# Reading wq in whole rows, a sigmoid on ScalarE and a bf16 residual in a decode kernel bound by its loads

## The chip, the cores and the metric

One core of one Trainium2 chip, the neighbouring cores idle. The metric is the device time of one execution in microseconds; lower is better. Executions of one kernel here spread by about 1%, so small differences are read from the traces (where the bytes were at what moment) and only totals from the timed runs.

## The reference, cut to what matters

Four tokens (batch 4, one position) pass twice through an attention layer and a gated layer, with residuals:

```python
def A(x, k_cache, v_cache, wq, wo):           # x after layer norm, [4, 512]
    q = x @ wq                                # wq: [512, 4096], bf16; 32 heads of 128
    k, v = last 2048 positions of the caches  # 8 kv heads, 4 query heads share one
    p = softmax(q @ k.T * 128**-0.5)
    return (p @ v) @ wo
def B(x, w_gate, w_up, w_down):               # 512 -> 1792 -> 512
    return (sigmoid(x @ w_gate) * (x @ w_up)) @ w_down
x = x + A(norm(x)); x = x + B(norm(x)); x = x + A(norm(x)); x = x + B(norm(x))
```

The same weights and caches serve both rounds. All of it, with what is read twice, comes to 72.36 MB of loads.

## The kernel before

All loads go through one queue (SyncE) into an arena of 50 slots of 512 KB (128 partitions x 4 KB). Each load takes a free slot; a slot comes free when the last instruction that reads it is done. The instructions of the five engines are planned by a list scheduler at build time; semaphores follow from that plan. K stays in the arena between the two attention layers, V and the weights are read again.

```python
wq_d = A_wq.rearrange("(kt p) n -> p kt n", p=128)      # block c: rows 128c .. 128c+127
...
# one load: half of each of 128 rows: 4 KB out of every 8 KB
chunk_load[("wq", c, i)] = lambda n, c=c, i=i: load_cols(
    n, wq_d[:, c, i * SLOT:(i + 1) * SLOT], SLOT, "bw_4k")
WQ_CH = [("wq", c, i) for i in range(2) for c in range(NC)]   # i outer: block 0,1,2,3 of half 0, then of half 1
...
def q_proj(k, b0, b1):
    for i in ((0, 1) if k == 0 else (1, 0)):                  # the query in two halves of 16 heads
        for c in range(NC):
            s = use_w("wq", k, ("wq", c, i))
            ...  # 4 matmuls of block c, half i; then done_w: the slot is free
        ...      # transpose, scale, replicate half i
...
# gated layer: sigmoid = 1 / (1 + exp(-g))
activation(egv, tv, ACTF.Exp, scale=-1.0)                     # ScalarE
tensor_scalar(eg, eg, 1.0, None, ALU.add)                     # VectorE
reciprocal(eg, eg)                                            # VectorE
tensor_tensor(hT, tv, egv, ALU.mult)                          # VectorE: times the up projection
...
# end: residual in f32, cast, transpose, copy, store
tensor_tensor(xT, ps, xT, ALU.add)
tensor_copy(xn, xT)                                           # the cast to bf16
```

## Time and profile before

| | before |
|---|---|
| timed, median (range, runs) | 192.74 us (192.09 to 193.40, 4) |
| profiled span | 190.2 us |
| loads | 72.36 MB; the load queue holds its 16 engines 97.9% of the span |
| busy share PE, DVE, ACT | 54%, 46%, 18% |

The span is the time on the core between first and last record; the timed figure is some 2 us longer. The profile's rows of slices cut the span into 40 parts; the row that matters here is the one of bytes per second. It stands under 400 where the packets are small (wo, in rows of 1 KB), it dips in the second slice and in the 27th, where the two passes over wq begin, and less in the 25th (371), where weights of the gated layer are read:

```profile
GB/s 133 344 416 410 408 410 389 409 394 404 407 390 411 391 405 412 388 409 394 400 393 389 407 405 371 397 337 409 409 409 408 402 410 406 408 408 405 403 365 16
```

Beside the profile's views I use one measure that comes from the packet records of the trace: the moment by which so many MB had arrived, counted from the first packet of the input x ("44 MB at 112.03 us").

### The profile page before, as it was taken

The numbers are of one execution on the slowest core, as the hardware profiler recorded it, in microseconds if no ns is written. First come the engines' busy times: TensorE is split into PE (matmuls) and PEld (weight loads), VectorE is DVE, ScalarE is ACT, GpSimd is POOL, SyncE is SP. The second block draws the span as 40 slices with busy tenths as digits, with TensorE's granted clock in tenths as the row PEclk, the third lists the DMA queues.
The fourth block names the chain that finished last, engine by engine and source line by source line (L and its number), as shares of the span: only waits on it lengthen the run. The fifth ranks groups of instructions, "written<-read, shape, count | busy, mean of one in ns | idle before, by whom it ended". The sixth has DMA issues, their size and how long they took to land.

```text
span 190.2 us, 4466 instructions
## 1 busy us (share of the span) xinstructions
PE 103.1 (54%) x1920; PEld 58.0 (30%) x1920; DVE 88.3 (46%) x220; ACT 33.3 (18%) x91; POOL 13.8 (7%) x73
## 2 busy tenths in 40 slices
PE   0443322655517264171654436445979999966543
PEld 0110000232404123041234331321355555655122
DVE  6136998486582854729410023122584443311421
ACT  2010011430303003030020000000373333310100
POOL 3000001110101001010010000000022111100000
PEclk9999999999999999999999999999995555555555
DMA  4999999999999999999999999999999999999990
GB/s 133 344 416 410 408 410 389 409 394 404 407 390 411 391 405 412 388 409 394 400 393 389 407 405 371 397 337 409 409 409 408 402 410 406 408 408 405 403 365 16
DMA packets 23412, 72.66 MB, mean 382 GB/s; under 512 B 2264, under 2 KB 6368, under 8 KB 23392
## 3 DMA queue, kind: packets, MB, share of 16 engines
q1 hardware_dynamic: 23392, 72.37, 97.9%
q8 instruction: 15, 0.25, 0.5%
q14 instruction: 5, 0.04, 0.1%
HBM read 72.36 MB, written 0.00 MB: 381 GB/s over the span
## 4 chain that ended last, share of the span: by engine, by line
SPq 52%; DMA 29%; PE 10%; issue 4%; DVE 3%; ACT 2%; ACTq 0%
SPq L369 51%; DMA arena<-in_A_v_cache_dram 13%; DMA arena<-in_B_w_down_dram 11%; DMA arena<-in_A_wq_dram 5%; PE ps L653 3%; PE ps L718 2%; ACT prow L670 1%; PE ps L808 1%; PE ps L679 1%; PE ps L840 1%; DVE nmax L661 1%; PE ps L580 1%; PE ps L748 1%; DVE ebuf L684 0%; DVE ebuf L588 0%
## 5 line engine op out<-in xcount | busy, mean ns | idle before, releaser
L653 PE MATMUL ps<-arena,qbd 128*16 128x512 bf16 x256 | 28.7, 594 | 30.3 <-DVE arena L633 26.5
L718 PE MATMUL ps<-ebuf,arena 128*128 128x4 bf16 x1024 | 34.3, 167 | 15.6 <-DMA arena<-in_A_v_cache_dram 10.9
L633 DVE STREAM_TRANSPOSE arena<-arena 128x1024 f32<-128x1024 f32 x32 | 38.6, 1226 | 0.6 <-DMA arena<-in_A_k_cache_dram 0.2
L718 PEld LDWEIGHTS ps<-ebuf,arena 128*128 128x128 bf16 x1024 | 31.4, 104 | 23.8 <-DMA arena<-in_A_v_cache_dram 21.8
L670 ACT ACTIVATE prow<-ps,nmax 128x512 bf16<-128x512 f32 x16 | 13.3, 829 | 42.7 <-DVE nmax L667 41.3
L653 PEld LDWEIGHTS ps<-arena,qbd 128*16 128x16 bf16 x256 | 6.4, 109 | 44.1 <-DVE arena L633 27.1
L730 DVE TENSOR_TENSOR onb<-ps,rinv 128x16 bf16<-128x16 f32 x16 | 3.1, 192 | 35.5 <-PE ps L718 35.4
L661 DVE TENSOR_REDUCE nmax<-ps 128x1 f32<-128x512 f32 x16 | 10.9, 683 | 15.3 <-PE ps L653 15.3
L621 ACT CAST qbd<-ps 32x64 bf16<-32x64 f32 x32 | 6.5, 203 | 48.7 <-DVE qbd L618 48.4
L580 PE MATMUL ps<-arena,xn 128*4 128x512 bf16 x64 | 9.3, 576 | 9.4 <-DMA arena<-in_A_wq_dram 6.5
L688 POOL CAST s<-psm 128x1 bf16<-128x1 f32 x16 | 3.0, 187 | 146.9 <-ACT prow L670 146.9
L679 PE MATMUL ps<-prow,perm 128*128 128x512 bf16 x16 | 9.0, 563 | 5.4 <-ACT prow L670 5.2
L681 ACT CAST prow<-ps 128x512 bf16<-128x512 f32 x16 | 9.4, 586 | 9.5 <-PE ps L679 9.5
L684 DVE STREAM_TRANSPOSE ebuf<-prow 128x256 f32<-128x256 f32 x16 | 7.1, 442 | 8.4 <-ACT prow L681 8.3
L748 PE MATMUL ps<-onb,arena 128*128 128x4 bf16 x256 | 9.3, 166 | 2.9 <-DVE onb L730 1.5
L808 PE MATMUL ps<-arena,xn 128*4 128x448 bf16 x64 | 7.3, 556 | 6.4 <-DMA arena<-in_B_w_up_dram 3.5
L618 DVE CAST qbd<-ps 32x64 bf16<-32x64 f32 x32 | 6.8, 212 | 5.1 <-ACT qbd L621 3.8
L748 PEld LDWEIGHTS ps<-onb,arena 128*128 128x128 bf16 x256 | 8.2, 104 | 3.2 <-issue 2.9
L547 ACT ACTIVATE lnv<-lnv 128x4 f32<-128x4 f32 x4 | 0.8, 206 | 39.3 <-DVE lnv L544 39.3
L588 DVE STREAM_TRANSPOSE ebuf<-ps 128x512 f32<-128x512 f32 x4 | 2.9, 714 | 9.8 <-PE ps L580 9.8
L840 PE MATMUL ps<-hT,arena 128*128 128x4 bf16 x112 | 4.2, 167 | 4.3 <-DVE hT L830 2.2
L815 DVE STREAM_TRANSPOSE ebuf<-ps 128x448 f32<-128x448 f32 x4 | 2.6, 650 | 7.9 <-PE ps L808 7.9
(55 smaller groups left out, 61.8 us busy)
## 6 DMA issues: line engine op xcount, KB each, us to landing
arena<-in_A_v_cache_dram SPq DMA_DIRECT2D x61, 512.0 KB, 12.6
arena<-in_A_k_cache_dram SPq DMA_DIRECT2D x32, 512.0 KB, 13.1
arena<-in_A_wq_dram SPq DMA_DIRECT2D x16, 512.0 KB, 8.6
arena<-in_A_wo_dram SPq DMA_DIRECT2D x8, 512.0 KB, 15.0
arena<-in_B_w_gate_dram SPq DMA_DIRECT2D x8, 448.0 KB, 13.9
arena<-in_B_w_up_dram SPq DMA_DIRECT2D x8, 448.0 KB, 13.7
arena<-in_B_w_down_dram SPq DMA_DIRECT2D x6, 512.0 KB, 10.2
arena<-in_B_w_down_dram SPq DMA_DIRECT2D x2, 256.0 KB, 10.3
```

What stands on the lines that cost most here:

```text
L369: o = P.op("sync", name, 0.0, lambda e, dst=dst, src=src: e.dma_start(dst, src), r=r, w=w, dma_bytes=nbytes, dma_rate=tm[rate])
L580: last = pe.matmul(ps[32 * hh:32 * hh + NB, qb, :], xn[:, c * NB:(c + 1) * NB], slot_ap(s)[:, hh * 512:(hh + 1) * 512], start=(c == 0), st ...
L633: P.op("vector", "T%d_%d" % (h, b), c_dve(1024), lambda v, v32=v32: v.transpose(v32, v32), r=[("slot", s)], w=[("slot", s)])
L653: last = pe.matmul(ps[32 * gi:32 * gi + NR, bank, :], qbd[:, q0:q0 + NR], kt[:, cp // 2, cp % 2, :, :], start=(cp == 0), stop=(cp == 3))
L661: lambda v: v.tensor_reduce(nmax[:, k2:k2 + 1], ps[:, bank, :], AXX, ALU.max),
L670: lambda a: a.activation(prow[:, :].rearrange("p (j k t) -> p j t k", k=32, t=2), ps[:, bank, :].rearrange("p (j t k) -> p j t k", k=32, t ...
L679: lambda pe: pe.matmul(ps[:, PB, :], perm[:, :], prow[:, :], start=True, stop=True),
L681: P.op("scalar", "pc" + tag, c_act(512), lambda a: a.copy(prow[:, :], ps[:, PB, :]), r=[("ppb",)], w=[("prow",)], banks=(PB,))
L684: lambda v: v.transpose(ebuf[:, k2 * 256:(k2 + 1) * 256], prow[:, :].bitcast(F32)),
L718: last = pe.matmul(ps[:, ob, gi * REP:(gi + 1) * REP], src[:, j * 128:(j + 1) * 128], ev[:, j % 2, j // 2, gi * REP:(gi + 1) * REP], start ...
L748: last = pe.matmul(ps[:, wb, c * nb:(c + 1) * nb], slot_ap(s)[:, r_ * D + c * 128:r_ * D + (c + 1) * 128], ov[:, o0:o0 + nb], start=(first ...
L808: last = pe.matmul(ps[32 * g:32 * g + NB, SB[n], 0:NF], xn[:, c * NB:(c + 1) * NB], slot_ap(s)[:, g * NF:(g + 1) * NF], start=(c == 0), st ...
```

## The change

The first pass over wq reads whole rows (8 KB) into two neighbouring slots, four loads of 1 MB in place of eight of 512 KB; the second pass stays as it was. The sigmoid becomes Exp, Ln(1 + .), Exp(-.), all on ScalarE. The last residual add writes bf16 directly, so the cast goes. The planner no longer counts a semaphore delay between two TensorE operations, which moves a few matmuls in the plan. (A field `lazy` is added to the planner and is zero everywhere.)

```diff
-                    td = d.finish + sem_lat
+                    td = d.finish + (0.0 if e == "tensor" and d.eng == e else sem_lat)
...
+        def load_wq_rows(c):
+            def emit(s):
+                assert pool.alloc() == s + 1
+                where[(("wq", c, 1), 0)] = s + 1
+                o = s * SLOT
+                dma("wqr%d" % c, arena[:, o:o + 2 * SLOT], wq_d[:, c, :], w=[("slot", s), ("slot", s + 1)],
+                    rate="bw_8k")
+            loads.append(((("wq", c, 0), 0), emit))
...
+            if kind == "wq" and k == 0:
+                for c in range(NC):
+                    load_wq_rows(c)
+                return
...
-            P.op("vector", "gp1%d" % k, c_dve(NH),
-                 lambda v: v.tensor_scalar(eg[:, 0:NH], eg[:, 0:NH], 1.0, None, ALU.add),
+            P.op("scalar", "gln%d" % k, c_act(NH),
+                 lambda a: a.activation(eg[:, 0:NH], eg[:, 0:NH], ACTF.Ln, bias=1.0),
...
-            P.op("vector", "grc%d" % k, c_dve(NH) + 250.0,
-                 lambda v: v.reciprocal(eg[:, 0:NH], eg[:, 0:NH]),
+            P.op("scalar", "grc%d" % k, c_act(NH),
+                 lambda a: a.activation(eg[:, 0:NH], eg[:, 0:NH], ACTF.Exp, scale=-1.0),
...
+            if last:
+                P.op("vector", "gres%d" % k, tm["dve_fix"] + 40.0,
+                     lambda v: v.tensor_tensor(xn[:, :], ps[:, CB, 128:128 + NX], xT[:, 0:NX], ALU.add),
+                     r=[("cb",)] + xts, w=[("xn",)], banks=(CB,))
+                return
...
-        P.op("vector", "out_cast", tm["dve_small"], lambda v: v.tensor_copy(xn[:, :], xT[:, 0:NX]),
-             r=[("xT", b) for b in range(NB)], w=[("xn",)])
```

More of the change, by code (lines that the diff above doesn't have):

```diff
@@ L17 @@
     __slots__ = ("idx", "eng", "name", "dur", "emit", "deps", "users", "start", "finish",
-                 "sem", "val", "inc", "dma_bytes", "dma_rate", "waits", "prio", "ndeps_left")
+                 "sem", "val", "inc", "dma_bytes", "dma_rate", "waits", "prio", "ndeps_left", "lazy")
     def __init__(self, idx, eng, name, dur, emit):
@@ L37, in __init__ @@
         self.ndeps_left = 0
+        self.lazy = 0.0
 class _Plan:
@@ L47, in __init__, with op @@
         self.bank_prev = {}
-    def op(self, eng, name, dur, emit, r=(), w=(), banks=(), dma_bytes=0, dma_rate=0.0, after=()):
+    def op(self, eng, name, dur, emit, r=(), w=(), banks=(), dma_bytes=0, dma_rate=0.0, after=(), lazy=0.0):
         o = _Op(len(self.ops), eng, name, dur, emit)
+        o.lazy = lazy
         o.dma_bytes = dma_bytes
@@ L125, in _schedule @@
                 ests.append((t, o))
-                if tmin is None or t < tmin:
-                    tmin = t
+                if tmin is None or t + o.lazy < tmin:
+                    tmin = t + o.lazy
             pick = None
             for x in ests:
-                if x[0] <= tmin + tol and (pick is None or x[1].prio < pick[1].prio):
+                if x[0] + x[1].lazy <= tmin + tol and (pick is None or x[1].prio < pick[1].prio):
                     pick = x
-            key = (pick[0], pick[1].prio)
+            key = (pick[0] + pick[1].lazy, pick[1].prio)
             if best is None or key < best_key:
@@ L263 @@
     dma_issue=60.0, dma_lat0=900.0, dma_lat1=1100.0, dma_max_out=16,
-    bw_4k=412.0, bw_3k=409.0, bw_1k=356.0,
+    bw_8k=430.0, bw_4k=412.0, bw_3k=409.0, bw_1k=356.0,
     pe_pair=38.0, pe_small=230.0, pe_f32=450.0, pe_row=80.0, pe_sq=300.0,
@@ L454, in build @@
                     last_use[(ch, v)] = k
+        def load_wq_rows(c):
[6 more added lines that the diff above has]
+            loads.append(((("wq", c, 0), 0), emit))
         def add_weights(kind, k, only=None):
+            if kind == "wq" and k == 0:
+                for c in range(NC):
+                    load_wq_rows(c)
+                return
             chs = chunks[kind]
-            if kind == "wq" and k:
+            if kind == "wq":
                 chs = chs[NC:] + chs[:NC]
@@ L791, in attn, with glu @@
                  r=[("psw", wb)] + [("xT", b) for b in g], w=[("xT", b) for b in g], banks=(wb,))
-        def glu(k, b0, b1):
+        def glu(k, b0, b1, last=False):
             nb = b1 - b0
@@ L892, in build @@
         g = GROUPS[-1]
-        glu(NG, g[0], g[-1] + 1)
+        glu(NG, g[0], g[-1] + 1, True)
         assert not loads
-        P.op("vector", "out_cast", tm["dve_small"], lambda v: v.tensor_copy(xn[:, :], xT[:, 0:NX]),
-             r=[("xT", b) for b in range(NB)], w=[("xn",)])
         def e_out_tr(pe):
```

## The prediction

> **What bounds the kernel now.** I read the engine shares first, then the slices, then the DMA issues, then stretches of four microseconds, then the end of the timeline.
>
> ```profile
> span 190.2 us, 4466 instructions
> ...
> PE 103.1 (54%) x1920; PEld 58.0 (30%) x1920; DVE 88.3 (46%) x220; ACT 33.3 (18%) x91; POOL 13.8 (7%) x73
> ...
> DMA  4999999999999999999999999999999999999990
> ...
> q1 hardware_dynamic: 23392, 72.37, 97.9%
> ...
> arena<-in_A_wq_dram SPq DMA_DIRECT2D x16, 512.0 KB, 8.6
> ```
>
> No compute engine is busy for much more than half of the span, while the DMA row is full from the second slice to the last but one, and the load queue alone holds its 16 engines for 97.9% of the span. 72.36 MB at the 410 GB/s of its steady stretches is 176.5 us. The rest of the 190.2 us is start, end, and places where the transfers ran below that rate. So a microsecond counts only if it is taken out of the transfers, out of the time before the first byte, or out of the time after the last. The chain of waits gives over half of its length to the issuing queue and another 29% to transfers, which agrees. The load queue is kept full: the median load lands 8.6 to 15 us after its issue, so a queue pause of a microsecond or two starves nothing.
>
> The stretches show where the rate sags (columns: stretch, length, PE, weight loads, DVE, ACT, POOL, clock, DMA share, GB/s):
>
> ```profile
> 4.00:8.00 4.00, 1.47 (x10) 0.71 (x10) 1.49 (x10) 0.41 (x2) 0.20 (x1) 1.00 0.89 286
> 8.00:12.00 4.00, 1.94 (x20) 0.30 (x20) 0.94 (x2) 0.00 (x0) 0.00 (x0) 1.00 1.01 413
> ...
> 124.00:128.00 4.00, 1.85 (x18) 0.85 (x16) 1.26 (x8) 0.41 (x2) 0.00 (x0) 1.00 0.96 324
> 128.00:132.00 4.00, 2.02 (x32) 0.52 (x28) 0.94 (x2) 0.00 (x0) 0.00 (x0) 1.00 1.01 412
> ```
>
> The two weakest stretches after the start-up are the ones in which a pass over wq begins, the first (4 to 8) and the second (124 to 128). In both the DMA share stays near 0.9 or above while the bytes fall, so the engines had packets in hand and each packet took longer. The packet records say the same: a 4 KB packet takes 159 to 160 ns in steady state, but most of those around 5 to 7 us and 125 to 126 us take 200 to 450 ns. The loss is (410-286)x4/410 = 1.2 us in the first pass and (410-324)x4/410 = 0.8 us in the second. Later wq chunks of the same shape run at full rate.
>
> The end, from the timeline:
>
> ```profile
> 185.97 1.00 PE L840 MATMUL ps<-hT,arena 128*128 128x4 bf16 x24 [0.67 <-DMA arena<-in_B_w_down_dram]
> 187.00 0.17 DVE L850 TENSOR_TENSOR xT<-ps,xT 128x16 f32<-128x16 f32 x1 [3.34 <-PE ps L840]
> 187.21 0.17 DVE L896 CAST xn<-xT 128x16 bf16<-128x16 f32 x1
> 187.44 0.30 PEld L902 LDWEIGHTS ps<-ident_b,xn 128*4 128x4 bf16 x4 [0.56 <-DVE xn L896]
> ```
>
> After the last w_down chunk lands, every instruction is on the path: 24 matmuls, the residual add, the cast, four transposes, a copy, the store.
>
> And the sigmoid of the last gated layer:
>
> ```profile
> 179.75 0.25 ACT L821 ACTIVATE eg<-ebuf 128x56 f32<-128x56 f32 x1 [2.75 <-DVE ebuf L815]
> ...
> 180.03 0.19 DVE L824 TENSOR_SCALAR eg<-eg 128x56 f32<-128x56 f32 x1 [0.32 <-ACT eg L821]
> 180.26 0.50 DVE L827 RECIPROCAL eg<-eg 128x56 f32<-128x56 f32 x1
> ...
> 182.76 0.65 DVE L815 STREAM_TRANSPOSE ebuf<-ps 128x448 f32<-128x448 f32 x1 [2.00 <-PE ps L808]
> 183.45 0.22 DVE L830 TENSOR_TENSOR hT<-ebuf,eg 128x56 bf16<-128x56 f32 x1
> ```
>
> The sigmoid is ready at 180.76; the product that uses it starts at 183.45, held by the transpose of the up projection, which is held by the arrival of w_up. It has 2.7 us of slack. In the first gated layer it is ready at 117.86 and used at 120.69, the same picture.
>
> **What the Trainium skill says.** (1) "DMA: Bandwidth & Descriptors", section "Why small descriptors are slow (HBM only)": each packet carries a fixed overhead of about 3 cycles, beside its bytes. The trace agrees in form: packets of 1, 2, 3.5 and 4 KB take 46, 84, 140 and 159 ns, a straight line of 0.0368 ns per byte plus 8.3 ns, so the fixed part is larger here. Eleven 8 KB packets of another queue take 310 ns at their quickest, on the same line (8.3 + 301.3). (2) The same page, section "Latency and other measured facts", has copies between HBM tensors running at half rate when the row pitch is a large power of two, 2 MiB and up being worst, with aliasing of channels as an unverified reason. The pitch of wq is only 8 KB and no run here has shown the cause, but half rows read at that pitch sagging to about 213 GB/s for some 2 us is what makes me take it seriously. (3) "ScalarE: Activation LUTs", section "Table sets: the hidden batching unit": exponential and logarithm share one set, so the new sequence needs no table switch; the trace of before has a single table load, at 0.81 us, and already alternates the two in its layer norms.
>
> **The change, part by part.**
> Whole rows of wq, first pass only: 8 loads of 512 KB in 4 KB packets become 4 loads of 1 MB. If a row travels as one 8 KB packet, 1024 packets become 512, so each of 16 engines has 32 packets fewer: 32 x 8.3 = 0.27 us off the transfers. This comes first in the queue and everything behind it is bound by transfers, so all of it should reach the end. On top, contiguous rows may remove the sag: up to 1.2 us, of which some is start-up that any load would pay. I take half of it, 0.6 us, as the expectation; it is a bet, not a calculation. The second pass keeps half rows and its 0.8 us.
> Against it: the first half of the query projection ended early before (its transpose began at 10.95 us); now both halves need the last row block, so both end near 16 us. The order of instructions shows two transposes of 0.72 us, two scalings of 0.22 and the copies into qbd now mixed with the transposes of K, some 2.8 us of VectorE work moved into a crowded time. First scores (21.81 before) come 3 to 4 us later. That delays when V slots come free, but the first slots are wanted much later than the first loads use them (50 slots, and eight of wq free early), and 8 to 15 us of loads are in flight. Cost: 0.
> Sigmoid: the two VectorE instructions (0.19 + 0.50) go, two ScalarE activations of 128x56 at about 0.25 each come in. Ready by about 180.5 instead of 180.76, not waited for: 0.
> Last residual in bf16: removes one cast of 0.17 us and its gap, 187.21 to 187.42, on the path that sets the end: 0.21 us.
> The scheduler no longer charges a delay between two TensorE operations. The order moves several V and score matmuls in the first attention layer; the second attention layer is almost unchanged. All of it lies behind full DMA engines: 0.
> Sum: 0.27 + 0.6 + 0.21 = 1.1 us; 192.8 - 1.1 = 191.7 us.
>
> **The rivals.**
> A, the sag stays or is a cold start: then only 0.27 + 0.21 = 0.5 us, 192.3 us. For it: the sag at the start is close to the first byte, when nothing is steady. Against it: the second pass sags with everything warm.
> B, the sag goes entirely: 0.27 + 1.2 + 0.21 = 1.7 us, 191.1 us. For it: both passes sag, and no K, V or w_down load, all contiguous, does so to this depth.
> C, the later queries become a new wait: K transposes at 1.23 us each nearly keep pace with K loads of 1.28 us, so 2.8 us of added work must be caught up. If V slots then came free too late, loads would be held: up to 2 or 3 us longer, 194 to 195 us. Against it: wo and V loads lie between groups of four K loads and leave VectorE free time, and the last V chunks of the first layer are awaited by TensorE, not the reverse.
> D, an 8 KB row is cut into 4 KB packets: the 0.27 falls away, the rest stands.
>
> **Range and chances.** A and B bound the likely outcome, 191.1 to 192.3; the three runs of before spread over 0.7 us, so I add 0.3 below and 0.6 above, the upper side being wider because of C: 190.8 to 192.9. Two per cent faster is 189.0, which would need 3.9 us, more than all the transfers' visible start-up loss; two per cent slower needs C at its worst. Hence 0.02 and 0.02.
>
> **What would show it.** Right: wq as 4 loads of 1 MB in the first pass, 512 packets of 8 KB near 310 ns; 4 to 8 us moving clearly more than 286 GB/s; the sag at about 123 us still there; no cast before the output transposes, whose start follows the residual add by 0.06 us; the sigmoid still ready over 2 us ahead of its product; a DMA row full throughout. Wrong: a stretch after 20 us with a DMA share well below 1 that before lacks, an unchanged rate between 4 and 8 us, or a total outside the range.

## The result, and the profile after

| | before | after | ratio, 95% interval |
|---|---|---|---|
| first comparison | 192.74 us (4 runs) | 189.99 us (4) | 0.9857, 0.9816 to 0.9899 |
| again (e5, below) | 192.48 us (15) | 189.99 us (4) | 0.9864, 0.9812 to 0.9915 |
| a third time (e11) | 192.24 us (11) | 190.01 us (6) | 0.9888, 0.9866 to 0.9911 |

A ratio is the mean time of one kernel's fast runs over that of the other's of the same rounds, so not quite the ratio of the medians quoted here. The gain is 2.2 to 2.75 us, 1.1 to 1.4%; forecast were 1.1 us. The direction was right and within 2%, the size was not, and 190.0 lies below the range of 190.8 to 192.9.

The page of the kernel after, the lines that answer to those of before (share and bytes by slice, the load queue, the issues of wq):

```profile
span 188.0 us, 4446 instructions
...
GB/s 158 424 420 412 411 407 389 410 390 408 405 394 408 388 412 404 392 410 392 399 395 389 408 407 370 368 405 417 405 412 404 406 405 410 405 407 404 406 374 26
...
q1 hardware_dynamic: 22816, 72.37, 98.3%
...
arena<-in_A_wq_dram SPq DMA_DIRECT2D x4, 1024.0 KB, 7.9
...
arena<-in_A_wq_dram SPq DMA_DIRECT2D x8, 512.0 KB, 7.7
```

The second slice went from 344 to 424 GB/s, the third from 416 to 420, and slices 4 to 24 are what they were. The dip of the 27th slice (337) is gone too (405); the 25th and 26th stand at 370 and 368, before at 371 and 397. The queue moves the same bytes in 576 fewer packets: 512 for the rows and 64 for the completions of four loads.

The stretches of four microseconds (same columns as in the prediction):

```profile
4.00:8.00 4.00, 1.62 (x10) 0.64 (x10) 1.50 (x10) 0.41 (x2) 0.20 (x1) 1.00 1.02 426
8.00:12.00 4.00, 1.93 (x17) 0.21 (x16) 0.00 (x0) 0.00 (x0) 0.00 (x0) 1.00 1.01 426
...
116.00:120.00 4.00, 1.65 (x28) 0.63 (x24) 0.87 (x2) 0.30 (x2) 0.00 (x0) 1.00 1.00 346
...
124.00:128.00 4.00, 2.01 (x18) 0.45 (x17) 0.70 (x5) 0.41 (x2) 0.00 (x0) 1.00 1.01 413
```

The last line is the second pass over wq, whose bytes begin to arrive at about 122 us here and 123 in before: it runs at 413 GB/s, where before had 324, although it still reads half rows. The third line is not wq. By their sizes (3.5 KB, then 4 and 2 KB) the packets from 114 to 122 us are those of the gated layer's weights. Their rate is low in both kernels: 377 and 346 GB/s in the two stretches from 112 us after, 391 and 371 before. It is not the sag of wq, as only about 1% of the 3.5 KB packets took over 200 ns; its cause was not pursued.

The end:

```profile
184.05 0.98 PE L855 MATMUL ps<-hT,arena 128*128 128x4 bf16 x24 [0.65 <-DMA arena<-in_B_w_down_dram]
185.06 0.17 DVE L866 TENSOR_TENSOR xn<-ps,xT 128x16 bf16<-128x16 f32 x1 [3.16 <-PE ps L855]
...
185.29 0.59 PE L919 MATMUL ps<-ident_b,xn 128*4 128x128 bf16 x4 [0.27 <-DVE xn L866]
```

From the residual add to the transposes it is 0.23 us now, 0.44 before (187.00 to 187.44): the 0.21 us of the cast.

The sigmoid of the last gated layer:

```profile
177.87 0.25 ACT L836 ACTIVATE eg<-ebuf 128x56 f32<-128x56 f32 x1 [2.75 <-DVE ebuf L830]
...
178.15 0.25 ACT L839 ACTIVATE eg<-eg 128x56 f32<-128x56 f32 x1
178.43 0.25 ACT L842 ACTIVATE eg<-eg 128x56 f32<-128x56 f32 x1
...
181.68 0.22 DVE L845 TENSOR_TENSOR hT<-ebuf,eg 128x56 bf16<-128x56 f32 x1
```

Ready at 178.68, used at 181.68: 3.0 us of slack, as unimportant as before.

Where the time came from, by bytes arrived (packet records; us). The last column is the rest of the span: the 1.75 us before the first packet of x, and all that follows the 72.3rd MB:

| kernel | wq in the first pass | 0 to 4.5 MB | 4.5 to 44 MB | 44 to 52 MB | 52 to 72.3 MB | rest |
|---|---|---|---|---|---|---|
| before | half rows | 13.29 | 98.73 | 21.09 | 50.75 | 6.30 |
| after | rows | 12.03 | 98.65 | 20.55 | 50.79 | 5.99 |
| difference | | -1.26 | -0.08 | -0.54 | +0.04 | -0.31 |

The first 4.5 MB are the first pass over wq and a little of K; 44 to 52 MB hold the gated layer's weights, up to about 47.7 MB, and then the second pass. Split there, the gated layer's part took 9.69 us before and 10.02 after, the second pass 11.39 and 10.54: the gain of that stretch lies in wq alone. The long stretches between are equal to a tenth of a microsecond. So the questions are: what about the rows makes the first pass faster, is the second pass's half microsecond chance, and do the other parts of the change do nothing?

### The profile page after: what moved, and what is told of

Same layout as the page of the kernel before. It is cut to its first block, busy times and chain, and to the rows that moved or that the text cites. A ratio compares the mean times of both kernels' runs of the same rounds, so it can differ in the third digit from the quotient of the medians.

```text
span 188.0 us, 4446 instructions
## 1 busy us (share of the span) xinstructions
PE 96.4 (51%) x1905; PEld 57.9 (31%) x1920; DVE 86.2 (46%) x215; ACT 34.3 (18%) x95; POOL 13.9 (7%) x73
## 4 chain that ended last, share of the span: by engine, by line
SPq 51%; DMA 29%; PE 10%; issue 4%; DVE 3%; ACT 2%; ACTq 0%
SPq L371 51%; DMA arena<-in_A_v_cache_dram 13%; DMA arena<-in_B_w_down_dram 11%; DMA arena<-in_A_wq_dram 4%; PE ps L668 4%; PE ps L733 2%; ACT prow L685 1%; PE ps L823 1%; PE ps L855 1%; DVE nmax L676 1%; PE ps L595 1%; PE ps L763 1%; DVE ebuf L699 0%; ACT qbd L636 0%; DVE ebuf L603 0%
## 5 line engine op out<-in xcount | busy, mean ns | idle before, releaser
L595 PE MATMUL ps<-arena,xn 128*4 128x512 bf16 x64 | 8.4, 593 | 8.1 <-DMA arena<-in_A_wq_dram 5.3
L713 PE MATMUL ps<-sel_b,s 128*128 128x16 bf16 x48 | 3.9, 179 | 8.9 <-POOL s L707 7.4
```

The lines of the kernel that those rows point to most:

```text
L595: last = pe.matmul(ps[32 * hh:32 * hh + NB, qb, :], xn[:, c * NB:(c + 1) * NB], slot_ap(s)[:, hh * 512:(hh + 1) * 512], start=(c == 0), st ...
```

## The experiments

Theory 1: the rows are the gain, through shorter transfers at the start; 1a: it is the order in which the bytes are read that removes the sag, and the longer packet adds 0.27 us. Rivals: the other parts of the change give some of it (2), a cold start that any first load pays (3), the packet size rather than the order (1b), the sequence of row blocks (1c), and that the second pass gains as a rule (4).

**e1: rows only.** The kernel before with `load_wq_rows` and nothing else of the change.

> The kernel before with nothing changed but the first pass over wq, read in whole rows. Theory 1 (the rows are the gain: shorter transfers at the start): 1 MB moved 1.0 us sooner than in before, wq and the K loads behind it 1.3 us sooner, no sag between 4 and 8 us; total 1.3 to 2.0 us below before. Rival 2 (the new order of TensorE or the sigmoid gives part of it): at most 0.9 us below before.

Measured: 190.63 us against 192.41, ratio 0.9919 (0.9888 to 0.9951), so 0.9 to 2.2 us less. The first 4.5 MB took 11.95 us, as in after (12.03), the stretch from 4 to 8 us ran at 424 GB/s. The rows alone bring the first pass's whole gain. (The total stays 0.6 us above the 189.99 and 190.01 that after had in other calls. The cast is 0.2 of that; the rest was not separated, and the intervals of the ratios overlap.)

**e2: all but the rows.** The kernel after, half rows in the first pass.

```diff
-                for c in range(NC):
-                    load_wq_rows(c)
+                for ch in chunks[kind]:
+                    chunk_load[ch]((ch, k))
```

> The kernel after with the first pass over wq read in half rows again, in the order of before. Theory 1: the sag between 4 and 8 us is back (about 286 GB/s there), only the cast's 0.2 us is left of the gain; total 0.1 to 0.5 us below before. Rival 2: over 0.9 us below before.

Measured: 192.41 us against 192.41, ratio 0.9999 (0.9978 to 1.0020; 22 runs, one of them slow and left out). The cast's 0.2 us is in its trace (0.22 us from residual add to transposes, against 0.44) but too small for the timing to show. The sag is back:

```profile
4.00:8.00 4.00, 1.32 (x10) 0.71 (x10) 1.49 (x10) 0.41 (x2) 0.20 (x1) 1.00 0.87 296
```

Rival 2 falls: the sigmoid on ScalarE and the new order of TensorE bring nothing that 22 runs can show. In the same direction: the stretch from 4.5 to 44 MB, in which the first attention layer runs in the new order, takes 98.65 to 98.73 us in all thirteen profiles of this study.

**e3: whole rows in 4 KB packets.** Each row goes to two slots that are not neighbours, so it needs two packets; load size and order stay.

```diff
-                assert pool.alloc() == s + 1
-                where[(("wq", c, 1), 0)] = s + 1
...
+                pool.free.remove(s + NC)
+                where[(("wq", c, 1), 0)] = s + NC
+                dst = arena[:, 0:2 * NC * SLOT].rearrange("p (h c n) -> p c h n", h=2, c=NC)[:, c]
...
```

> The kernel after, whole rows of wq in loads of 1 MB, but each row lands in two slots that are not neighbours, so it travels as two packets of 4 KB. Theory 1a (the order in which the bytes are read removes the sag, the longer packet only saves 0.27 us): no sag, rate of the wq stretch about 410 to 415 GB/s, total 0.2 to 0.4 us above after. Rival 1b (the 8 KB packet removes the sag): the sag is back, total about 1.3 us above after.

Measured: 190.56 us, ratio to before 0.9926; no sag:

```profile
4.00:8.00 4.00, 1.62 (x10) 0.64 (x10) 1.49 (x10) 0.41 (x2) 0.20 (x1) 1.00 1.03 421
8.00:12.00 4.00, 1.31 (x12) 0.21 (x16) 0.00 (x0) 0.00 (x0) 0.00 (x0) 1.00 1.03 415
```

From 0.25 to 4.5 MB it took 10.22 us, after takes 9.95 and before 11.60. So the order is worth 1.4 us against before, and the longer packet the 0.27 us that the prediction worked out, to the digit. The packets of after agree: 512 of them have 8 KB, with a median of 309 ns. Some of the order's worth is paid back at the start: the first quarter of a MB is there at 2.47 us in e3, at 2.08 in after, at 1.69 in before. Theory 1a stands, 1b falls.

Two limits. The total was to lie 0.2 to 0.4 us above after, which did not run in this call; beside after's 189.99 and 190.01 of other calls it lies 0.6 above, as the first 4.5 MB do in the traces (12.69 against 12.03). And e3, like after, has four loads of 1 MB where before has eight of 512 KB; whole rows in loads of 512 KB were not tried. Against the size alone speaks that K, in contiguous loads of 512 KB, runs at full rate (e7).

**e4: half rows, in row order.** Eight loads as before, but the two halves of a block one after the other.

```diff
-                for c in range(NC):
-                    load_wq_rows(c)
+                for c in range(NC):
+                    for i in range(2):
+                        chunk_load[("wq", c, i)]((("wq", c, i), k))
```

> The kernel after, but wq in the first pass as eight loads of half rows, the two halves of a block of 128 rows one after the other. Each load alone still reads 4 KB of every 8 KB. Theory 1a with the pitch inside a load as the cause: the sag stays, about 286 GB/s between 4 and 8 us, total about 1.3 us above after. Rival 1c (the cause is which block follows which, as the sag falls in the second load, on another block of rows): no sag in the second load, total 0.3 to 0.5 us above after.

Measured: 191.46 us, ratio to before 0.9962 (0.9944 to 0.9980), about half of the gain of e1. The loss is there, but spread:

```profile
4.00:8.00 4.00, 1.19 (x6) 0.62 (x6) 1.49 (x10) 0.41 (x2) 0.20 (x1) 1.00 0.98 362
8.00:12.00 4.00, 2.22 (x16) 0.28 (x16) 0.00 (x0) 0.00 (x0) 0.00 (x0) 1.00 1.00 378
```

In the packet records its slow packets come three times, near 0.5, 1.25 and 2.25 MB, each time near the step to the next load or block. The first 4.5 MB took 13.11 us, 1.1 more than in after, and the total lies 1.5 us above after's of other calls, near the 1.3 that 1a expected; the place of the loss and its depth (286 GB/s) are not as 1a had them, and 1c is not right either. Loads that each read half rows lose time even when their neighbour reads the other half, somewhat less than in the order of before (13.14 to 13.65 us in the other kernels with half rows).

**e7: K first.** e2 with four loads of K ahead of wq.

```diff
+        loads[:] = loads[8:12] + loads[0:8] + loads[12:]
         fill()
```

> The kernel after with half rows of wq in the first pass, and four loads of K put ahead of wq. Theory 1a (half rows sag wherever they begin): the first 2 MB (K) run at full rate once begun, 4 KB packets at 160 ns, and about 1 us is lost in the first MB or so of wq behind them. Rival 3 (a cold start that any first load pays): the K loads lose the 1 us and wq behind them loses less than 0.3 us.

Measured (one execution): the K loads run at full rate, the sag comes when wq comes:

```profile
4.00:8.00 4.00, 0.59 (x2) 0.50 (x2) 3.72 (x8) 0.00 (x0) 0.20 (x1) 1.00 1.02 412
8.00:12.00 4.00, 0.59 (x4) 0.12 (x4) 2.16 (x7) 0.41 (x2) 0.00 (x0) 1.00 1.02 292
```

The packets of the third MB took 1.1 us more (of 16 engines) than at their usual 159 ns; those of the first two MB 0.5 us, nearly all of it in the first quarter, which is what after pays there as well (0.46). Rival 3, the cold start, falls. In the prediction I had let it keep half of its chance.

**e8: blocks in the order 2, 3, 0, 1.** Half rows, two halves as before.

> The kernel after with half rows of wq in the first pass, blocks of 128 rows in the order 2, 3, 0, 1. If the sag belongs to the place in the sequence (the second load of a run of half rows): the slow packets come between 0.5 and 1.1 MB moved, as before. If it belongs to the rows 128 to 255 of wq: they come between 1.6 and 2.1 MB moved.

Measured (one execution): 271 GB/s from 4 to 8 us, the slow packets between 0.25 and 1.25 MB, as in before. The sag sits around the second load of a run of half rows, whichever rows those are.

**e10: half rows alternating with K.** Against e2:

```diff
+        loads[0:16] = [loads[(j // 2) + 8 * (j % 2)] for j in range(16)]
         fill()
```

> The kernel after with half rows of wq in the first pass, each followed by one K load. If the sag needs two loads of half rows one behind the other: excess time of packets in the first 4 MB below 0.6 us, little more than the start of any kernel costs (0.2 to 0.5 us). If each change into half rows costs something by itself: 1 us or more.

Measured (one execution): 333 GB/s from 4 to 8 us; packets of the first 4 MB took 1.3 us more than usual, in two lumps (0.25 to 0.5 MB and 1.25 to 2 MB). So a K load between them does not take the sag away: it does not need two loads of half rows back to back.

One more control lies in every trace. w_down is read 4 KB out of every 14 KB of a partition's rows (the prediction calls it contiguous, which it is not), and in the last layer none of its packets took over 172 ns in 12 of the 13 profiles; a few did in e9. So a load that takes a part of each row is not slow as such.

**e5 and e11: after, again.** Unchanged, for the second pass.

> The kernel after, unchanged, to have it beside more runs of before and to see a second profile. Theory 1 (first pass -1.3 us, end -0.2 us, what was more than that in the first comparison came from how the second pass over wq happened to run): 1.4 to 2.2 us below before; between 44 and 52 MB moved the transfers take anything from 20.5 to 21.4 us, as they did over the six profiles so far. Rival 4 (the change also helps the second pass): 20.5 us again in that stretch, and 2.2 us or more below before.

> The kernel after, unchanged, as the partner of e9 and for a third profile of its second pass over wq. Theory 1: 1.4 to 2.6 us below before; 44 to 52 MB moved in 20.5 to 21.4 us. Rival 4 (the change helps the second pass as a rule): again below the 20.9 us that no profile of a half-row kernel has gone under.

Measured: the totals are in the table of the result; e5's stretch was 20.96 us, not the 20.5 of rival 4. The stretch 44 to 52 MB, whose second half is the second pass, by kernels whose second pass is the same half rows:

| first pass in | 0 to 4.5 MB, us | 44 to 52 MB, us |
|---|---|---|
| half rows: before, e2, e4, e7, e8, e10 | 13.29, 13.65, 13.11, 13.14, 13.55, 13.16 | 21.09, 21.36, 20.91, 21.06, 21.24, 22.04 |
| rows: after, e5, e11, e1, e3 | 12.03, 12.00, 12.01, 11.95, 12.69 | 20.55, 20.96, 20.29, 20.94, 20.58 |

Five against six with means of 20.66 and 21.28, and they overlap only at 20.91 to 20.96. Part of the stretch is the gated layer's weights, which do not separate the two groups (44 to 47.7 MB: 9.60 to 10.11 us with rows, 9.69 to 10.58 with half rows). The second pass itself does (47.7 to 52 MB): 10.54, 11.01, 10.67, 10.79, 10.67 us with rows, 11.39, 11.07, 11.09, 11.37, 11.00, 11.45 with half rows, in the order of the table.

It looks like rival 4: where the first pass reads rows, the second pass, unchanged, sags less. I have no mechanism that I could show. The queue's longest wait between 97 and 131 us is the same in all eleven profiles (7.7 to 7.8 us, for a matmul of the gated layer), and in the second pass the packets took 0.1 to 0.6 us (of 16 engines) more than usual with rows, 0.5 to 1.1 with half rows, so it is the packets and not the issue. Nor is it the slots that wq takes in the first pass: e4 has those of after, e3 those of before. e11 expected 20.9 at most by this rival and had 20.29; but single profiles vary by half a microsecond, and five against six is a tendency rather than a proof.

**e6: both passes in rows.** Second pass: four loads of 1 MB into any two free slots.

```diff
...
+                near = [t for t in pool.free if abs(t - s) == 1]
+                s2 = near[0] if near else pool.free[0]
...
(in fill)
-            while loads and pool.free:
+            while loads and len(pool.free) >= (2 if loads[0][0][0][0] == "wq" else 1):
```

> The kernel after with the second pass over wq in whole rows too: four loads of 1 MB into pairs of free slots, one pair of neighbours (8 KB packets), three pairs apart (two 4 KB packets a row). Theory 1a (half rows are what sags): the second sag goes, 44 to 52 MB in 20.2 us or less, total 0.4 to 1.0 us below after. Rival: the sag of the second pass comes from the issue that waits for slots, or from what follows the gated layer; then it stays and the total is that of after or worse, as loads wait for two slots at a time.

Measured: 192.55 us, ratio to before 0.9995: the whole gain is lost. The second sag is gone (420 GB/s from 124 to 128 us), yet 44 to 52 MB took 20.82 us and not the 20.2 that 1a expected: 10.12 for the gated layer's part and 10.70 for the second pass, no less than behind a first pass in rows with half rows in the second. And behind it the engines run dry: the DMA share of 0.70 is the lowest of any such stretch in the middle of a span here.

```profile
124.00:128.00 4.00, 1.66 (x14) 0.57 (x18) 0.70 (x5) 0.41 (x2) 0.00 (x0) 1.00 1.01 420
...
132.00:136.00 4.00, 1.17 (x20) 0.25 (x24) 1.03 (x3) 0.00 (x0) 0.00 (x0) 1.00 0.70 265
```

Who held the queue, 112 to 140 us (waiter, released by, us in total, times, longest):

```profile
SPq L371 <- PE ps L616: 10.7, 4, 3.6
```

L616 is the query projection itself. The slots that the gated layer had freed did not suffice for four pairs: the queue was busy with the four issues from 117.28 to 127.04 us, and the last went out only after the first block of wq had been multiplied (125.86 to 126.88). The loads of V stood behind it in the queue. The MB from 52 to 53 arrived in 3.96 us, where all others but e9 (2.8) take 2.5.

**e9: rows for three blocks, halves for the fourth.** So that nothing waits for two slots that wq itself must free. Against e6:

```diff
-                for c in range(NC):
+                for c in range(NC - 1):
                     load_wq_rows2(c, k)
+                for i in (1, 0):
+                    chunk_load[("wq", NC - 1, i)]((("wq", NC - 1, i), k))
```

> The kernel after with the second pass over wq as three loads of whole rows (two slots each) and the last block of rows as two half loads, so that no load waits for two slots that only wq itself can free. Theory 1a (half rows sag, and the hole of run e6 at 52 to 53 MB was the fourth pair waiting for slots): no hole, 44 to 52 MB in 20.5 us or less, total 0.3 to 0.8 us below after of the same call. Rival (what the sag gives back is lost in slots anyway): a hole again behind wq, total as after or above.

Measured: 190.57 us, ratio to before 0.9911 (0.9884 to 0.9938); its partner after 190.01, 0.9888. The stretch 44 to 52 MB took 20.23 us, the shortest of all, and what follows gave it back: 128 to 132 at 391 GB/s, 132 to 136 at 365, 136 to 140 at 381, where e11 has 413, 409 and 408. The transfers from 52 to 72.3 MB took 51.05 us against 50.75 in e11. What slowed these later transfers I did not pursue.

Most of the loss is not in the transfers, though. The last bytes of the weights landed at 184.11 us in e9 and 183.89 in e11, 0.2 us apart; the spans are 1.1 us apart (188.82 and 187.72). First e9, then e11:

```profile
179.79 3.16 PE L848 MATMUL ps<-arena,xn 128*4 128x448 bf16 x32 [1.42 <-DVE xn L598]
...
184.19 1.63 PE L880 MATMUL ps<-hT,arena 128*128 128x4 bf16 x56 [1.24 <-DVE hT L870]
```

```profile
175.17 2.04 PE L823 MATMUL ps<-arena,xn 128*4 128x448 bf16 x20 [1.43 <-DVE xn L573]
...
183.74 1.00 PE L855 MATMUL ps<-hT,arena 128*128 128x4 bf16 x24 [0.65 <-DMA arena<-in_B_w_down_dram]
```

In e11 the last matmuls wait for the last load. In e9 the last gated layer starts 4.6 us later, all its matmuls run without a wait for a load, and 0.9 us more is left to do after the last byte: the end of this kernel is set by the engines and not by the loads. Why its second attention layer ended later was not pursued. So e9 is not better than after, which remains the best version found.

## Why the prediction was wrong, point by point

- **The bound.** Right. The loads fill the span, before and after; what moved the time of after moved bytes or the end. (In e9 the engines set the end.)
- **The first failing step:** "I take half of it, 0.6 us, as the expectation; it is a bet, not a calculation." That contiguous rows remove the sag was right; the size was not. The runs show the term whole: order alone is worth 1.4 us from 0.25 MB on (e3 against before), less what the first quarter of a MB comes later (0.4 us in after, 0.8 in e3). Net of both and with the packets, 0 to 4.5 MB shrank by 1.26 us, where 0.87 was forecast. The half came from rival A, a cold start; e7 removes it. The profile of before had already held the evidence against A, since the second pass sags warm; I gave it too little weight. The 1.2 us was also measured on one mild execution: other kernels with half rows in that order needed 13.55 and 13.65 us for the first 4.5 MB (e8, e2), before 13.29, so the typical gain is nearer 1.5 us than 1.26.
- **The second failing step:** "The second pass keeps half rows and its 0.8 us." It keeps half rows, but not the loss: from 47.7 to 52 MB the packets took 0.79 us (of 16 engines) more than usual in before and 0.13 in after. With the gated layer's part, 44 to 52 MB were 0.54 us shorter in the profiled pair, 0.6 us in the mean of five against six profiles. So "the sag at about 123 us still there", named as a sign of being right, did not come in this profile. Of the 2.15 us between the two spans 1.1 were forecast; of the other 1.1, 0.4 is the first step's and 0.5 this one's. This is the larger surprise, and its cause stays open.
- **The starting value.** 192.8 us was the median of three runs of before. Later calls give 192.24 to 192.48 (69 runs), so a part of the first comparison's 2.75 us is luck. From these values the forecast would have been 191.1 to 191.4, still above the 190.0 measured.
- **Two readings.** Of the 4 KB packets that start from 5 to 7 us, 39% take 200 to 450 ns, and 46% from 125 to 126 us: many, but not "most". And 187.42, as the end of the cast's gap, is 187.44 in the trace.
- **8 KB packets, 0.27 us.** Right: 512 packets with a median of 309 ns, 0.27 us between e3 and after.
- **The cast, 0.21 us.** Right in the trace; invisible in the timing of e2.
- **Sigmoid, 0; scheduler, 0.** Right as far as e2 can tell (0.9978 to 1.0020).
- **Rival C, later queries.** Its worth was right (0; 4.5 to 44 MB are unchanged) but its size was wrong: first scores were to come 3 to 4 us later, and came at 22.25 instead of 21.81, because the whole pass ends 1.8 us sooner (last query matmuls at 13.58 instead of 15.41) and other things set the moment: in before the K transposes on VectorE, in after the copy of the query into qbd (done at 22.19), whose VectorE half had stood in line among those transposes.
- **The range.** Its lower edge was rival B less 0.3 us, that is the whole sag of one profile, and no allowance for the sag of the second pass, though I had just seen that it exists and had no account of its cause. The sum of what the runs show, 1.3 to 1.5 for the first pass, 0.5 to 0.7 for the second, 0.2 for the end, is 2.0 to 2.4 us, beside 2.2 to 2.75 timed.

## What to carry to other kernels

In a kernel bound by loads, look for stretches where the DMA share is full and the bytes per second are not: there the packets are slow, and the shape of the read is worth changing, even at equal packet size. First make sure, by the order of the queue and the packet sizes, whose bytes a slow stretch holds. Read contiguous rows where the slots allow it, but count the slots: a load that needs two at once can starve the queue and cost more than the faster read gives (e6), and the engines can come to set the end (e9). And when one profile shows a loss without a known cause, neither halve it for safety nor take its size from one execution: a reordering of loads, such as e7's, is cheap and tells a cold start from a pattern.

## What the Trainium skill lacked or had wrong

- "DMA: Bandwidth & Descriptors", section "Specifications", gives 512 B as the least transfer for line rate. Here the packets reach 22 GB/s an engine at 1 KB (46 ns), 25.8 at 4 KB (159 ns) and 26.5 at 8 KB (309 ns): a step from 4 to 8 KB still saves 3%, 0.27 us on 4 MB. The fixed part in the section "Why small descriptors are slow (HBM only)", about 3 cycles, is 8.3 ns here; at the measured 0.0368 ns a byte and the page's 32 B a cycle that is about 7 cycles (an estimate).
- The same page, section "Latency and other measured facts", tells of slow row pitches from 2 MiB up (164 GB/s at 2 MiB, half rate at 4 and 8 MiB). Reading 4 KB of every 8 KB row cost 1.4 us on 4 MB here (e3 against before), in a burst around the second load of a run (down to about 213 GB/s for some 2 us), after which the same pattern ran at 410 GB/s. No page has that, and these runs do not show its cause.
- No page has what the first quarter of a MB costs: it was there at 1.65 to 1.87 us in the six profiles with first loads of 512 KB, at 1.89 to 2.08 in the six with loads of 1 MB in 8 KB packets, at 2.47 in e3.
- No page says how little TensorE's clock matters when loads bound: e7 was granted 0.50 of full speed from 24 to 112 us, where before has 1.00, and its stretch from 4.5 to 44 MB took 98.67 us, before's 98.73.
